# Cosine attention and a GELU layer on one core: two score passes moved in front of the next w_in stage

## The chip, the core and the metric

The kernel runs on one core of a Trainium2 chip. The metric is the time of one execution in microseconds of the device; smaller is better. The kernel before takes 417.93 us as the median of its first three runs. All runs used are fast, with a granted TensorE clock of 0.992 to 1.0.

## The reference

Shapes: q, k, v are (8 batches, 12 heads, 448 positions, 64), x is then (3584, 768), w_in (768, 2048), w_out (2048, 768).

```python
q_n = q / (np.linalg.norm(q, axis=-1, keepdims=True) + 1e-06)
k_n = k / (np.linalg.norm(k, axis=-1, keepdims=True) + 1e-06)
attn = softmax(np.matmul(q_n, k_n.transpose(0, 1, 3, 2)) / tau)      # tau = 0.1 (written out in the original)
out = np.matmul(attn, v)
x = out.transpose(0, 2, 1, 3).reshape(B * S, H * D)
h = x @ w_in
g = 0.5 * h * (1.0 + erf(h / np.sqrt(2.0)))
return g @ w_out
```

## The kernel before

One batch after the other goes through attention (`attention(b)`) and the first matmul with its gelu (`first(b)`, called the w_in stage here). The second matmul (w_out) of earlier batches is cut into single matmuls, and these *fill* the gaps of the next batch's attention: `run()` issues a number of them from a plan. The order on each engine is the order in which the program issues. (The code below leaves out loads, squares and scales.)

The profile names the work by the tiles: st is a pass of scores, pt its exps, sm the row sums, o the values, hp the w_in stage, op the w_out matmuls, nq a reduced square. "Turn" is used in two ways. A turn of TensorE is its change from one kind of matmul to another; VectorE's turn of the sums (tr) is the transpose that takes them out of their bank.

A batch has three *quads* of four heads. A quad has seven *passes*: a pass is four 64x64 matmuls into a pair of PSUM banks (`scores`) and one exp of that pair on ScalarE (`exps`). A *visit* is a few passes in a row. After a quad's seven passes come its row sums, its values and its normalising (`both`).

```python
    def both(g, p):
        sums(g)                  # TensorE, 16 matmuls into one of the two small banks
        turned(g)                # VectorE: transposes the sums out of that bank
        inverted(g)
        spread(g, 0)
        spread(g, 1)
        values(g, p=p)           # TensorE, 28 matmuls into pair p
        normalise(g, 0)          # VectorE: writes x, which the w_in stage reads
        normalise(g, 1)

    group_pairs = [(0, 1, 2), (0, 1, 2), (0, 1, 2), (1, 2), (1, 2, 0), (1, 2, 0), (2, 0), (2, 0)]
    # ... group(b, k) issues the passes of the k-th visit into these pairs ...

    def attention(b, fill):
        plan = {96: (20, 13, 13, 12, 16, 22), 128: (24, 18, 20, 18, 22, 26)}[len(fill)]
        # ...
        run()
        # ... scale and transpose the third quad ...
        group(b, 1)
        run()
        group(b, 2)
        both(g0, 0)
        group(b, 3)
        run()
        group(b, 4)
        run()
        group(b, 5)
        both(g0 + 1, 1)
        group(b, 6)
        run()
        group(b, 7)
        upto(reduce, nu + 2)     # VectorE; ScalarE's logs and roots of the next norms follow
        # ...
        run()
        both(g0 + 2, 1)
        # ...

    def first(b):
        # ...
        pairs = (0, 2) if b else (0, 2, 6, 8)     # which hp banks come from the big pairs
        ahead = 4 if b else 5                      # w_in columns begun before the last quad's x is read
        # ... 96 matmuls, 16 gelus ...
        nc.scalar.preload_act_table_set(EXP_SET)
        group(b + 1, 0)          # the first visit of the next batch: behind the w_in stage
        upto(root, 2 * b + 6)
```

The kernel uses eight PSUM banks: three pairs (0, 1, 2) and two single ones, the "small" ones, that the w_out matmuls, the sums and some w_in columns take in turn. There are 15 tiles for exps, 4 for loaded q and k, 3 for transposed quads. Batches are counted from 0. The fill has 96 matmuls in batches 1, 3, 5 and 7, and 128 in 2, 4 and 6.

Of the kernel before, what the change touches and what calls it, by code (L numbers as in the profile page):

```python
# [16 lines left out]
def kernel(  # L17
# [20 lines left out]
    NQ = H // 4  # L38
# [66 lines left out]
    def pair(i, name):  # L105
        pool = third[0] if i == 2 else ps_st
        return pool.tile([128, 2, 512], F32, tag=f"st{i}", name=name)
# [3 lines left out]

    units = [(0, 0, 1), (0, 1, 2)] + [(g, 0, 2) for g in range(1, NG)]
    NU = len(units)
    groups = [[n] for n in range(NQ + 2)] + [[NQ + 2, NQ + 3]]
    for n in range(2 * NQ + 1, NU, NQ):
        groups += [[n, n + 1], [n + 2]]
    shapes = [[len(gr), 2, units[gr[0]][2] - units[gr[0]][1], C] for gr in groups]
    place = {u: (n, j) for n, gr in enumerate(groups) for j, u in enumerate(gr)}
    qk_t, v_t, sq_t, nq_t, rn_t, qkb_t, qkT_t, pt_t = {}, {}, {}, {}, {}, {}, {}, {}
# [139 lines left out]
    def sums(g, chunks=range(C)):  # L259
        for c in chunks:  # L260
            if c == 0:
                bank_t[g, "sm"] = ps_acc.tile([128, 512], F32, tag="sm", name=f"sm{g}") if g < NQ else \
                    mm_tile(f"sm{g}", aside=0)
            for s in range(2):
                if g < NQ:
                    nc.tensor.matmul(bank_t[g, "sm"][64 * s:64 * (s + 1), :S],  # L266
                                     lhsT=ones2.rearrange("p a h r -> p (a h r)"), rhs=pt_t[g, s, c],
                                     start=(c == 0), stop=(c == C - 1), tile_position=(0, 64 * s))
                    continue

                half = 2
                for i in range(2) if c == half else ((c - (c > half)) % 2,):
                    r = 32 * (2 * s + i)
                    cols = slice(i * S // 2, (i + 1) * S // 2) if c == half else slice(0, S)
                    nc.tensor.matmul(bank_t[g, "sm"][r:r + 32, cols], lhsT=ones, rhs=pt_t[g, s, c][:, cols],  # L275
                                     start=(c < 2), stop=(c >= C - 2), tile_position=(0, r))
# [18 lines left out]
    def turned(g):  # L295
        tr = rcp.tile([128, NB, 32], F32, tag="tr", name=f"tr{g}")
        nc.vector.transpose(tr.rearrange("p b r -> p (b r)"), bank_t.pop((g, "sm"))[:, :S])  # L297
        bank_t[g, "tr"] = tr.rearrange("p b (k r) -> p k b r", k=2)

    def inverted(g):  # L300
        tr = bank_t.pop((g, "tr"))
        if g < NQ:
            su = tr[:, :, :, 0]
        else:


            for j in range(4):
                o = j ^ 1
                nc.vector.tensor_reduce(tr[32 * j:32 * (j + 1), :, :, 1], tr[32 * o:32 * (o + 1), :, :, 0:1],  # L309
                                        mybir.AxisListType.X, ALU.add)  # L310
            su = rcp.tile([128, 2, NB], F32, tag="su", name=f"su{g}")
            nc.vector.tensor_reduce(su, tr[:, :, :, 0:2], mybir.AxisListType.X, ALU.add)
        rc = bank_t[g, "rc"] = rcp.tile([128, 2, NB], F32, tag="rc", name=f"rc{g}")
        nc.vector.reciprocal(rc, su)

    def spread(g, h):
        rs = rcp.tile([128, NB, 32], F32, tag=f"rs{h}", name=f"rs{g}_{h}")
        nc.vector.transpose(rs, bank_t[g, "rc"][:, h].to_broadcast([128, NB, 32]))  # L318
        rs_t[g, h] = rs.rearrange("p b r -> p (b r)")
# [5 lines left out]
    def both(g, p):  # L325
        sums(g)
        turned(g)
# [3 lines that stand above are left out]
        values(g, p=p)  # L331
        normalise(g, 0)
        normalise(g, 1)
# [60 lines left out]
    def upto(f, n, last=None):  # L394
        last = {load_qk: NG, load_v: NV, root: len(groups), load_wi: 4, load_wo: 4}.get(f, NU)
        while done.get(f, 0) < min(n, last):
            done[f] = done.get(f, 0) + 1
            f(done[f] - 1)
# [173 lines left out]
        done.update({square: 6, reduce: 5, root: 5, scale: 5, transposes: 5})  # L572


    passes = [(n, c) for n in range(NQ) for c in range(C)]
    group_pairs = [(0, 1, 2), (0, 1, 2), (0, 1, 2), (1, 2), (1, 2, 0), (1, 2, 0), (2, 0), (2, 0)]

    def group(b, k):
        n0 = sum(len(p) for p in group_pairs[:k])
        for p, (n, c) in zip(group_pairs[k], passes[n0:]):  # L580
            scores(b * NQ + n, ((0, c), (1, c)), p)
            exps(b * NQ + n, ((0, c), (1, c)))

    def attention(b, fill):
        fill = list(fill)
        plan = {96: (20, 13, 13, 12, 16, 22), 128: (24, 18, 20, 18, 22, 26)}[len(fill)]
        parts = iter(plan)

        def run():
            for _ in range(next(parts)):  # L590
                fill.pop(0)()

        x_t[b] = xp.tile([128, KD, S], BF16, tag="x", name=f"x{b}")
        g0, nu = b * NQ, (b + 1) * NQ + 1
        run()
        for n in (nu - 1, nu):
            upto(scale, n)
            upto(transposes, n)
        group(b, 1)
        upto(square, nu + 1)  # L600
        run()
        group(b, 2)
        both(g0, 0)
        upto(load_v, b + 3)
        if b == 1:
            upto(load_qk, g0 + NQ + 2)
        group(b, 3)
        upto(square, nu + 2)
        run()
        group(b, 4)  # L610
        upto(reduce, nu + 1)
        upto(load_qk, g0 + NQ + 3)
        run()
        group(b, 5)
        both(g0 + 1, 1)
        group(b, 6)
        run()
        group(b, 7)
        upto(reduce, nu + 2)
        n = 2 * b + 4  # L620
        if n < len(groups):
            logs(n)
            roots(n)
        run()
        both(g0 + 2, 1)
        if n < len(groups):
            inverses(n)
            done[root] = n + 1

    def first(b):  # L630
        sb, hf = divmod(b, 2)
        if hf == 0:
            g_t[sb] = gp.tile([128, KF, 2 * S], BF16, tag="g", name=f"g{sb}")
        nc.scalar.preload_act_table_set(GELU_SET)
        nu = (b + 1) * NQ + 1
        hps = {}
        pairs = (0, 2) if b else (0, 2, 6, 8)
        ahead = 4 if b else 5

        def mm(m, kds):  # L640
            for kd in kds:
                nc.tensor.matmul(hps[m], lhsT=wi[:, kd, m * 128:(m + 1) * 128],  # L642
                                 rhs=x_t[b][:, kd, :], start=(kd == 0), stop=(kd == KD - 1))

        def bank(m):
            if m in pairs:
                p = (2, 0)[m // 2] if b else (1, 0, 1, 0)[pairs.index(m)]
                st = pair(p, f"hp{b}_{m}")
                hps[m], hps[m + 1] = st[:, 0, :S], st[:, 1, :S]
            elif m not in hps:  # L650
                hps[m] = mm_tile(f"hp{b}_{m}")[:, :S]

        for m in range(ahead):
            bank(m)
            mm(m, range(KD - 2))
        if b == 0:
            upto(square, nu + 3)
        for n in (nu + 1, nu + 2) if b else (nu + 1,):
            upto(scale, n)
            upto(transposes, n)  # L660
        if b:
            upto(load_qk, (b + 1) * NQ + 5)
        else:
            upto(load_wo, 4)
        upto(square, nu + 3)
        upto(reduce, nu + 3)
        for m in range(ahead):
            mm(m, range(KD - 2, KD))
        for m in range(KF):
            if b == 0 and m == 8:  # L670
                for i in range(2):
                    transposes(4, i)
                    copies(4, i)
            if m >= ahead and (m == 0 or m - 1 not in pairs):
                for k in range(m, m + 1 + (m in pairs)):
                    bank(k)
                    mm(k, range(KD))
            nc.scalar.activation(g_t[sb][:, m, hf * S:(hf + 1) * S], hps.pop(m), AF.Gelu)  # L678
            if b == 0 and m == 5:
                nc.scalar.preload_act_table_set(EXP_SET)  # L680
                upto(root, 6)
                nc.scalar.preload_act_table_set(GELU_SET)
                upto(scale, nu + 2)
                upto(transposes, nu + 2)
                upto(load_qk, 2 * NQ + 1)
        if b + 1 < B:
            nc.scalar.preload_act_table_set(EXP_SET)
            group(b + 1, 0)
            upto(root, 2 * b + 6)

    upto(load_qk, 1)
# [8 lines left out]
    fill = []  # L700
    for b in range(B):
# [12 lines left out]
        fill = [f for t, ni in todo if t not in tail for f in second_pieces(sb, t, ni)]  # L714
# [38 lines left out]
```

## Time and profile before

| Engine | busy us of 416.8 |
|---|---|
| TensorE | 409.3 |
| ScalarE | 246.6 |
| VectorE | 188.3 |
| GpSimd | 167.3 |

TensorE's "busy" is nearly the span, so it tells little about how well the engine is used: the same 12 matmuls of a visit count 0.69 us in one place and 0.82 in another. The chain of waits in order of time is of more use, because it gives each stretch of matmuls its own length. The same work can then be compared in two places, and what one of them takes longer is a wait or a turn. The prediction below shows the lines for batch 3.

### The profile page before, as it was taken

The page shows a single profiled execution, that of the slowest core. Times are in us where ns is not written, and L with a number is a line of the kernel's source. Part 1 is how long each engine was busy: PE and PEld are TensorE (multiplying, and loading weights), DVE is VectorE, ACT ScalarE, POOL GpSimd, SP SyncE. Part 2 cuts the span into 40 slices and gives each one's busy share as a digit, 9 for nine tenths or more (in the row PEclk, how much of TensorE's full clock was granted, in tenths as well). Part 3 has the DMA queues.
Part 4 walks back from the last instruction along what each step waited for, and adds up shares of the span by engine and source line. Part 5 has one row for each costly group of instructions (what it writes and reads, how often), then busy time and mean ns, then how long its engine had stood idle before and what let it go on. Part 6 is the DMA issues. An engine that isn't in the chain of part 4 may idle for free.

```text
span 416.8 us, 8254 instructions
## 1 busy us (share of the span) xinstructions
PE 409.3 (98%) x3506; PEld 212.1 (51%) x3506; DVE 188.3 (45%) x379; ACT 246.6 (59%) x358; POOL 167.3 (40%) x113
## 2 busy tenths in 40 slices
PE   7899999999999999999999999999999999999996
PEld 3344545555555554554555555455555554555564
DVE  5777228801676016741276314861167511661021
ACT  5995698356663578735865359735866348844300
POOL 4999706090900909053640636317280272000000
PEclk9999999999999999999999999999999999999999
DMA  8999999445473546729192382936375160430033
GB/s 288 263 259 205 204 215 258 115 81 186 91 185 77 92 174 92 187 60 242 18 233 65 77 228 43 195 77 126 141 135 180 38 90 0 85 75 2 0 77 76
DMA packets 66516, 54.53 MB, mean 131 GB/s; under 512 B 38576, under 2 KB 61488, under 8 KB 66480
## 3 DMA queue, kind: packets, MB, share of 16 engines
q1 hardware_dynamic: 53984, 41.79, 39.3%
q0 software_dynamic: 12112, 11.80, 17.8%
q8 instruction: 27, 0.44, 0.4%
q10 hardware_dynamic: 384, 0.43, 0.3%
q14 instruction: 9, 0.07, 0.1%
HBM read 45.61 MB, written 11.01 MB: 136 GB/s over the span
## 4 chain that ended last, share of the span: by engine, by line
PE 95%; DMA 2%; ACT 1%; DVE 1%; SPq 1%; issue 0%; DVEq 0%
PE hp L642 35%; PE op L352 35%; PE st L246 9%; PE o L289 8%; PE sm L275 4%; DMA qk<-in_q_dram 2%; PE op L367 1%; PE sm L266 1%; ACT pt L253 1%; SPq L129 1%; PE tp L225 0%; DVE qkT L230 0%; ACT sq L154 0%; DVE rn L192 0%; ACT root L178 0%
## 5 line engine op out<-in xcount | busy, mean ns | idle before, releaser
L253 ACT ACTIVATE pt<-st 128x896 bf16<-128x896 f32 x168 | 143.0, 917 | 39.6 <-PE st L246 38.7
L352 PE MATMUL op<-wo,g 128*128 128x384 bf16 x864 | 147.9, 327 | 0.0
L642 PE MATMUL hp<-x,wi 128*128 128x448 bf16 x768 | 146.8, 353 | 0.0
L678 ACT ACTIVATE g<-hp 128x448 bf16<-128x448 f32 x128 | 66.8, 547 | 99.3 <-PE hp L642 99.0
L352 PEld LDWEIGHTS <-g 128*128 128x128 bf16 x864 | 81.1, 98 | 63.2 <-issue 12.7
L642 PEld LDWEIGHTS <-wi 128*128 128x128 bf16 x768 | 74.4, 98 | 71.4 <-issue 2.9
L208 POOL TENSOR_TENSOR qkb<-qk,rn 128x896 bf16<-128x896 f32 (+1 forms) x49 | 79.7, 1652 | 47.1 <-DVE rn L192 47.1
L165 DVE TENSOR_REDUCE nq<-sq 128x28 f32<-128x1792 f32 (+2 forms) x30 | 48.8, 1637 | 64.6 <-POOL sq L156 61.3
L156 POOL TENSOR_TENSOR sq<-qk 128x1792 f32<-128x1792 f32 (+1 forms) x22 | 66.8, 3042 | 12.9 <-DMA qk<-in_k_dram 12.7
L356 DVE COPY ot<-op 128x384 f32<-128x384 f32 x54 | 29.5, 547 | 69.6 <-PE op L352 69.6
L190 POOL TENSOR_SCALAR se<-sr 128x28 f32<-128x28 f32 (+1 forms) x14 | 4.4, 313 | 122.7 <-ACT sr L181 122.7
L246 PE MATMUL st<-qkT 64*64 64x448 bf16 x672 | 48.3, 359 | 1.2 <-DVE qkT L230 1.0
L289 PE MATMUL o<-pt,v 64*64 64x448 bf16 x672 | 36.9, 352 | 0.0
L246 PEld LDWEIGHTS <-qkT 64*64 64x64 bf16 x672 | 18.2, 105 | 26.6 <-issue 18.3
L192 DVE RECIPROCAL rn<-se 128x28 f32<-128x28 f32 (+2 forms) x18 | 6.8, 376 | 51.4 <-POOL se L190 51.1
L318 DVE STREAM_TRANSPOSE rs<-rc 128x448 f32<-128x448 f32 x48 | 28.1, 623 | 0.8
L297 DVE STREAM_TRANSPOSE tr<-sm 128x448 f32<-128x448 f32 x24 | 15.6, 649 | 28.5 <-PE sm L275 25.4
L323 DVE TENSOR_TENSOR x<-o,rs 128x448 bf16<-128x448 f32 x48 | 27.0, 600 | 1.0 <-DVE rs L318 0.5
L289 PEld LDWEIGHTS <-v 64*64 64x64 bf16 x672 | 17.7, 106 | 15.8 <-issue 7.2
L275 PE MATMUL sm<-pt,ones 128*32 128x448 bf16 (+1 forms) x336 | 19.3, 332 | 0.0
L309 DVE TENSOR_REDUCE tr<-tr 32x28 f32<-32x28 f32 x84 | 16.5, 196 | 1.6
L275 PEld LDWEIGHTS <-ones 128*32 128x32 bf16 x336 | 7.4, 95 | 10.6 <-issue 8.9
(43 smaller groups left out, 118.5 us busy)
## 6 DMA issues: line engine op xcount, KB each, us to landing
out_dram<-ot SPq DMA_DIRECT2D x54, 192.0 KB, 2.7
qk<-in_q_dram SPq DMA_DIRECT2D x23, 448.0 KB, 6.3
qk<-in_k_dram SPq DMA_DIRECT2D x23, 448.0 KB, 7.0
v<-in_v_dram POOLq DMA_DIRECT2D x7, 672.0 KB, 10.8
wi<-in_moe_w_in_dram POOLq DMA_DIRECT2D x8, 384.0 KB, 14.3
wo<-in_moe_w_out_dram POOLq DMA_DIRECT2D x4, 768.0 KB, 14.0
qk<-in_q_dram SPq DMA_DIRECT2D x2, 224.0 KB, 3.6
v<-in_v_dram POOLq DMA_DIRECT2D x1, 448.0 KB, 9.5
```

The costliest lines, as they stand in the source:

```text
L156: eng.tensor_tensor(sq[:, part], t[:, part], t[:, part], ALU.mult)
L165: nc.vector.tensor_reduce(nq[:, part], sq[:, part], mybir.AxisListType.X, ALU.add)
L208: eng.tensor_tensor(qkb[:, i, :, s0:s1].rearrange("p c s d -> p s c d"), t[:, i, s0:s1], rn[:, i].to_broadcast([128, s1 - s0, C, D]), ALU. ...
L246: nc.tensor.matmul(st[cols, n, :S], lhsT=qkT[rows, 1, c, cols], rhs=qkT[rows, 0, :, cols], start=True, stop=True, tile_position=(64 * s, 6 ...
L253: nc.scalar.activation(pt[:, :m], st[:, :m, :S], AF.Exp, scale=inv_tau)
L275: nc.tensor.matmul(bank_t[g, "sm"][r:r + 32, cols], lhsT=ones, rhs=pt_t[g, s, c][:, cols], start=(c < 2), stop=(c >= C - 2), tile_position ...
L289: nc.tensor.matmul(bank_t[g, h][cols, :S], lhsT=v_t[g][rows, s, c, :], rhs=pt_t[g, s, c][rows], start=(c == 0), stop=(c == C - 1), tile_po ...
L318: nc.vector.transpose(rs, bank_t[g, "rc"][:, h].to_broadcast([128, NB, 32]))
L352: nc.tensor.matmul(ps[:, :NH], lhsT=g_t[sb][:, kf, t * 128:(t + 1) * 128], rhs=wo[:, kf, ni * NH:(ni + 1) * NH], start=(kf == 0), stop=(kf ...
L356: nc.vector.tensor_copy(ot[:, ni * NH:(ni + 1) * NH], ps[:, :NH])
L642: nc.tensor.matmul(hps[m], lhsT=wi[:, kd, m * 128:(m + 1) * 128], rhs=x_t[b][:, kd, :], start=(kd == 0), stop=(kd == KD - 1))
L678: nc.scalar.activation(g_t[sb][:, m, hf * S:(hf + 1) * S], hps.pop(m), AF.Gelu)
```

## The change

Intent: from the fourth batch on, two score passes of a batch are issued before the w_in stage of the batch in front of it, right behind that batch's last values. The visit behind the w_in stage goes, the other visits are spread anew among the w_out matmuls, and the norms and transposes run one quad further ahead. The w_in stage takes other banks first, and begins six columns instead of four before it reads the last quad.

```diff
-    groups = [[n] for n in range(NQ + 2)] + [[NQ + 2, NQ + 3]]
-    for n in range(2 * NQ + 1, NU, NQ):
-        groups += [[n, n + 1], [n + 2]]
+    groups = [[n] for n in range(NQ + 2)] + [[NQ + 2, NQ + 3], [2 * NQ + 1, 2 * NQ + 2]]
+    for n in range(3 * NQ, NU, NQ):
+        groups += [[n, n + 1], [n + 2]] if n + 2 < NU else [[n]]
 ...
-        plan = {96: (20, 13, 13, 12, 16, 22), 128: (24, 18, 20, 18, 22, 26)}[len(fill)]
+        plan = {96: (16, 14, 16, 18, 16, 16), 128: (20, 18, 20, 22, 32, 16)}[len(fill)]
 ... attention(b), visits, runs and sums alone:
-        run(); group(b, 1); run(); group(b, 2); both(g0, 0); group(b, 3); run()
-        group(b, 4); run(); group(b, 5); both(g0 + 1, 1); group(b, 6); run(); group(b, 7)
-        run(); both(g0 + 2, 1)
+        run(); visit(b, (0, 1, 2)); run(); visit(b, (0, 1, 2)); run()
+        visit(b, (0, 1) if b <= 2 else (0, 1, 2)); run()
+        visit(b, (0, 1, 2)); both(g0, 0); visit(b, (1, 2)); run()
+        visit(b, (1, 2, 0)); both(g0 + 1, 1); visit(b, (2, 0)); run()
+        both(g0 + 2, 2)
+        if b > 1:
+            visit(b + 1, (0, 1))
 ... first(b):
-        pairs = (0, 2) if b else (0, 2, 6, 8)
-        ahead = 4 if b else 5
+        pairs = {2: 0, 4: 1} if b else {0: 1, 2: 0, 6: 1, 8: 0}
+        ahead = 6 if b else 5
 ...
-            group(b + 1, 0)
+            if b <= 1:
+                visit(b + 1, (0, 1, 2))
```

(The lines of the attention are drawn together here; the loads, squares, reduces and scales between them move too.)

More of the change, by code (lines that the diff above doesn't have):

```diff
@@ L575, with visit @@
     passes = [(n, c) for n in range(NQ) for c in range(C)]
-    group_pairs = [(0, 1, 2), (0, 1, 2), (0, 1, 2), (1, 2), (1, 2, 0), (1, 2, 0), (2, 0), (2, 0)]
-    def group(b, k):
-        n0 = sum(len(p) for p in group_pairs[:k])
-        for p, (n, c) in zip(group_pairs[k], passes[n0:]):
+    at = {}
+    def visit(b, pairs):
+        for p in pairs:
+            n, c = passes[at.get(b, 0)]
+            at[b] = at.get(b, 0) + 1
             scores(b * NQ + n, ((0, c), (1, c)), p)
@@ L593, in attention @@
         x_t[b] = xp.tile([128, KD, S], BF16, tag="x", name=f"x{b}")
-        g0, nu = b * NQ, (b + 1) * NQ + 1
+        g0, u = b * NQ, b * NQ + 1
         run()
-        for n in (nu - 1, nu):
-            upto(scale, n)
-            upto(transposes, n)
-        group(b, 1)
-        upto(square, nu + 1)
-        run()
-        group(b, 2)
+        upto(scale, u + 3)
+        upto(transposes, u + 3)
+        if b == 1:
+            upto(load_qk, g0 + NQ + 2)
+            upto(square, u + 4)
+        visit(b, (0, 1, 2))
+        if b > 1:
+            upto(scale, u + 4)
+            upto(transposes, u + 4)
+        run()
+        visit(b, (0, 1, 2))
+        run()
+        upto(load_qk, g0 + NQ + 3)
+        visit(b, (0, 1) if b <= 2 else (0, 1, 2))
+        upto(square, u + 5)
+        run()
+        visit(b, (0, 1, 2))
         both(g0, 0)
         upto(load_v, b + 3)
-        if b == 1:
-            upto(load_qk, g0 + NQ + 2)
-        group(b, 3)
-        upto(square, nu + 2)
+        upto(load_qk, g0 + NQ + 4)
+        visit(b, (1, 2))
+        upto(reduce, u + 4 + (b > 1))
         run()
-        group(b, 4)
-        upto(reduce, nu + 1)
-        upto(load_qk, g0 + NQ + 3)
-        run()
-        group(b, 5)
+        visit(b, (1, 2, 0))
         both(g0 + 1, 1)
-        group(b, 6)
-        run()
-        group(b, 7)
-        upto(reduce, nu + 2)
+        visit(b, (2, 0))
+        upto(reduce, u + 5)
         n = 2 * b + 4
@@ L624, in attention @@
         run()
-        both(g0 + 2, 1)
+        both(g0 + 2, 2)
         if n < len(groups):
@@ L628, in attention @@
             done[root] = n + 1
+            if b > 1:
+                visit(b + 1, (0, 1))
     def first(b):
@@ L634, in first @@
         nc.scalar.preload_act_table_set(GELU_SET)
-        nu = (b + 1) * NQ + 1
+        u = (b + 1) * NQ + 1
         hps = {}
-        pairs = (0, 2) if b else (0, 2, 6, 8)
-        ahead = 4 if b else 5
+        pairs = {2: 0, 4: 1} if b else {0: 1, 2: 0, 6: 1, 8: 0}
+        ahead = 6 if b else 5
         def mm(m, kds):
@@ L646, in bank @@
             if m in pairs:
-                p = (2, 0)[m // 2] if b else (1, 0, 1, 0)[pairs.index(m)]
-                st = pair(p, f"hp{b}_{m}")
+                st = pair(pairs[m], f"hp{b}_{m}")
                 hps[m], hps[m + 1] = st[:, 0, :S], st[:, 1, :S]
@@ L656, in first @@
         if b == 0:
-            upto(square, nu + 3)
-        for n in (nu + 1, nu + 2) if b else (nu + 1,):
-            upto(scale, n)
-            upto(transposes, n)
-        if b:
+            upto(square, u + 3)
+            upto(scale, u + 1)
+            upto(transposes, u + 1)
+            upto(load_wo, 4)
+            upto(reduce, u + 3)
+        else:
+            upto(scale, u + 2)
+            upto(transposes, u + 2)
             upto(load_qk, (b + 1) * NQ + 5)
-        else:
-            upto(load_wo, 4)
-        upto(square, nu + 3)
-        upto(reduce, nu + 3)
+            upto(square, u + 4)
+            upto(reduce, u + 4)
         for m in range(ahead):
@@ L682, in first @@
                 nc.scalar.preload_act_table_set(GELU_SET)
-                upto(scale, nu + 2)
-                upto(transposes, nu + 2)
+                upto(scale, u + 2)
+                upto(transposes, u + 2)
                 upto(load_qk, 2 * NQ + 1)
```

## The prediction

> **What bounds the kernel now.** I read the page's engine table first (TensorE busy 409.3 of 416.8 us at a granted clock of 0.998), then the chain of waits by line, then the same chain in order of time.
>
> ```profile
> PE 95%; DMA 2%; ACT 1%; DVE 1%; SPq 1%; issue 0%; DVEq 0%
> PE hp L642 35%; PE op L352 35%; PE st L246 9%; PE o L289 8%; PE sm L275 4%; DMA qk<-in_q_dram 2%; PE op L367 1%; PE sm L266 1%; ACT pt L253 1%; SPq L129 1%; PE tp L225 0%; DVE qkT L230 0%; ACT sq L154 0%; DVE rn L192 0%; ACT root L178 0%
> ```
>
> The chain is TensorE from 19 us to the end, so time comes only from what stands between one matmul and the next on that engine. The number of matmuls does not change (3506). What can change is how often TensorE turns from one kind of matmul to another and where it waits for a bank. The chain in time shows both. Here is batch 3 (counting from 0), columns start us, length us, what:
>
> ```profile
> 131.99 18.27 PE hp L642 x96
> 150.26 0.69 PE st L246 x12
> 150.95 3.36 PE op L352 x20
> 154.31 0.82 PE st L246 x12
> 155.12 2.22 PE op L352 x13
> 157.34 0.72 PE st L246 x12
> 158.06 0.98 PE sm L275 x16
> 159.04 1.45 PE o L289 x28
> 160.49 0.38 PE st L246 x8
> 160.87 2.22 PE op L352 x13
> 163.09 0.79 PE st L246 x12
> ...
> 171.98 0.50 PE st L246 x8
> ...
> 176.16 0.78 PE sm L275 x16
> ```
>
> Three things are to be seen. First, a price of turning: two passes (8 matmuls) cost 0.38 us right behind the values (o, the same 64x64 tiling) and 0.50 us behind w_out matmuls (op, 128x128): 0.12 us for the turn. In the same chain 13 op matmuls take 2.22 us and 26 take 4.33 us, so one is 0.162 us and the turn into op 0.11 us; 96 op matmuls behind the w_in stage (hp, also 128x128) take 15.60 us, which is 0.1625 each and no turn at all. Second, waits: three passes cost 0.69 us when nothing is short, but 0.82, 0.72 and 0.79 us in this batch. Third, the first row sums (sm) of a batch take 0.98 us, the later ones 0.78 us.
>
> ScalarE's timeline tells why (start, length, what):
>
> ```profile
> 150.86 1.28 ACT L687 ACT_TABLE_LOAD   x1
> 152.15 2.54 ACT L253 ACTIVATE pt<-st 128x896 bf16<-128x896 f32 x3
> 154.56 0.33 ACT L172 ACTIVATE lq<-nq,tiny 128x28 f32<-128x28 f32 x1
> 155.11 5.13 ACT L253 ACTIVATE pt<-st 128x896 bf16<-128x896 f32 x6
> ```
>
> The first visit's scores are ready at 151, but the last gelu and the table load hold its exps until 152.15; they free the third pair of banks only near 154.7, and the second visit, begun at 154.31, has to wait for it. Its own exps wait for the logs and run into the third visit's (six in a row). The sums need seven passes; the seventh is the first of the third visit, started 0.7 us earlier, and its exp ends about 0.2 us too late.
>
> **What the Trainium skill says.** "TensorEngine Tiling (Array Packing)", Key Properties: changing the tiling mode drains the TensorE. The trace agrees: 0.11 to 0.12 us a change, nothing from o to st or from hp to op. "ScalarE: Activation LUTs", What ACT_TABLE_LOAD costs: about 1283 ns for a load; the trace has 1.28. "PSUM — Partial Sum Buffer", Engine vs sequencer instructions: VectorE's queue is strict FIFO; the trace agrees in that its rows never overtake the built order, and my loss below rests on it.
>
> **The change, part by part.** (a) In batches 3 to 7 the visit behind the w_in stage is gone. Two of its passes stand behind the last values of the batch before, and hp runs straight into op. Counting turns per batch: 19 before, 17 after; five batches, so 10 x 0.12 = 1.2 us.
>
> (b) The first sums come after four visits (14 passes from batch 3 on), not after three: all seven exps are long done. 0.20 to 0.23 us in each of seven batches: 1.5 us.
>
> (c) The run of op between visits is 14 to 18 in the batches with 96 op matmuls (1, 3, 5, 7), where it was 12, 13 and 13, and the exps that start a batch are no longer behind a table load. In batches 3, 5 and 7 the 0.13 + 0.03 + 0.10 us of waits go: 0.8 us. In exchange the two-pass visit behind the first values gets as close to its exps as the one behind the second values is now, which takes 0.42 us and not 0.38: 0.04 x 7 = 0.3 us lost.
>
> (d) Batches 1 and 2 keep the visit behind w_in, now with only 16 and 20 op behind it (20 and 24 before). Its exps end 4.5 us after w_in. In batch 1 the next visit starts 0.69 + 2.71 = 3.4 us after w_in and waits 0.6 us for its third pair; in batch 2, 0.1 us.
>
> Summing the pieces with the durations above gives these stretches from w_in to w_in: 46.40 us becomes 45.77 in batches 3 and 5 and 45.39 in batch 7 (whose two passes left and which sends none ahead); 51.37 becomes 51.68 in batch 2 (it takes in two passes) and 50.97 in batches 4 and 6. Batches 2 to 7: 293.31 before, 290.55 after, 2.76 us won. Batch 1 up to its w_in stage: 28.13 becomes 28.3.
>
> (e) The hidden part. The w_in stage now takes its first two banks from the two small ones, and the last row sums stand in the very bank that it takes first. So it cannot start before VectorE has turned those sums. VectorE's timeline of batch 1 before the change:
>
> ```profile
> 74.44 2.00 DVE L165 TENSOR_REDUCE nq<-sq 128x28 f32<-128x1792 f32 x1
> 76.36 0.55 DVE L356 COPY ot<-op 128x384 f32<-128x384 f32 x1
> 78.43 0.56 DVE L356 COPY ot<-op 128x384 f32<-128x384 f32 x1 [1.52 <-PE op L352]
> 79.22 0.65 DVE L297 STREAM_TRANSPOSE tr<-sm 128x448 f32<-128x448 f32 x1 [0.23 <-PE sm L275]
> ```
>
> Now there is slack (the brackets: idle time before the row, and what ended it): 38 op matmuls lie between the second values and the last sums. After the change there are 16. In batch 1 a reduce still stands in between. I follow VectorE's order from the first sums' end at an estimated 68.0 us. Turn and normalise take 4.29 us to the next start, reduce 1.92, copy 0.55, so the second turn starts near 74.8, although its sums ended at 74.0. Then 4.29, reduce 1.92, copy 0.5: the third turn runs from 81.5 to 82.15. TensorE is through with the values at 80.85 and waits 1.35 us. With the 0.2 us from (d), batch 1 loses 1.6 us. From batch 2 on the second of these reduces is gone (one stands behind the first values, two in the w_in stage). In batch 3 the third turn then ends about 1.0 us before w_in needs the bank. Normalising the last quad also stays ahead: 24 instead of 16 matmuls run before it is needed.
>
> Net: -2.76 + 1.6 = -1.2 us.
>
> **Rivals.** First, the wait in (e) doesn't arise or isn't this long: then about 415.3 us. For it: ready times are estimates. Against: the built order has TensorE wait for VectorE at the first hp matmul, and before the change it doesn't. Second, (e) also bites in batches 3, 5 and 7. The slack is only 1.0 us, and a reduce that starts late would bring it back; 1 us in each would give 419.8. Against: that reduce's square comes from GpSimd about 5 us before it is wanted. Third, the exp waits of (b) and (c) only move, so that turns alone are won: 417.9 - 1.2 + 1.6 = 418.3. Against: after w_in ScalarE has its logs behind it at 2.6 us, and the first visit comes no sooner. Fourth, a buffer runs short. Fourteen exp tiles are outstanding before the first values, of 15; that fits, but a late release would stop ScalarE. The quad ahead needs its turned tile's buffer, free after the second visit, and a transfer that took 2.6 us before with over 10 us to spare: hidden.
>
> **Range and chances.** From the median of 417.93 us I predict 416.7. The gain of 2.8 is a sum of small terms, each good to about a third; the loss is one term, between 0.5 and 2. Eight times in ten: 415.0 to 418.2. Two per cent is 8.4 us; no rival gets there short of a deadlock-like wait in every batch. Faster by over 2%: 0.01; within 2%: 0.97; slower: 0.02.
>
> **What would show it.** In the chain of the changed kernel: no st between hp and op from batch 3 on; every three-pass visit there at 0.69; every first sum at 0.78; the stretches 45.8 and 51.0 us; a w_in stage of batch 1 that starts near 82.2 us, with a gap before it that ends on VectorE's turn of the sums. I am wrong if such gaps come in later batches, if sums stay at 0.98, or if batch 1 starts its w_in stage near 80.8.

## The result, and the profile after

The changed kernel takes 416.97 us (median of six runs, 416.80 to 417.30), the kernel before 418.16 us in the six runs beside it. The ratio is 0.9971, with a 95% interval of 0.9958 to 0.9984. By the limit of 2% that is "same"; the interval lies below one, so a small gain is there.

The chain of waits of the changed kernel in order of time, batch 3 (start us, length us, what):

```profile
151.60 2.60 PE op L352 x16
154.20 0.69 PE st L246 x12
154.89 2.38 PE op L352 x14
157.28 0.69 PE st L246 x12
...
164.40 0.69 PE st L246 x12
165.09 0.78 PE sm L275 x16
165.87 1.45 PE o L289 x28
167.31 0.42 PE st L246 x8
...
178.70 0.38 PE st L246 x8
179.08 18.27 PE hp L649 x96
```

The w_out matmuls stand right behind the w_in stage, which ended at 151.60, and 16 of them take 2.60 us, 0.1625 each, so that join is free of a turn. Every visit of three passes takes 0.69 us. The first sums take 0.78. The two passes ahead cost 0.38 us behind the values.

Batch 1 looks different. TensorE's timeline there, with the idle time before a row in brackets:

```profile
55.23 0.72 PE L246 MATMUL st<-qkT 64*64 64x448 bf16 x8
56.38 0.38 PE L246 MATMUL st<-qkT 64*64 64x448 bf16 x4 [0.43 <-ACT pt L253]
...
78.92 1.52 PE L289 MATMUL o<-pt,v 64*64 64x448 bf16 x28
81.61 4.70 PE L649 MATMUL hp<-x,wi 128*128 128x448 bf16 x24 [1.16 <-DVE tr L297]
```

and VectorE's timeline of the same place:

```profile
78.54 2.00 DVE L165 TENSOR_REDUCE nq<-sq 128x28 f32<-128x1792 f32 x1
80.45 0.54 DVE L356 COPY ot<-op 128x384 f32<-128x384 f32 x1
80.92 0.63 DVE L297 STREAM_TRANSPOSE tr<-sm 128x448 f32<-128x448 f32 x1
```

The sums had ended near 79.0 us, when the values began. VectorE turned them out of their bank only at 80.92, because a reduce and a copy stood in front of the turn in its queue. The w_in stage wanted that bank next, and TensorE stood still for 1.16 us. VectorE was late before that: the chain of waits of this batch runs on VectorE from 67.60 us, the turn of the first sums, to 81.56, with no pause over 0.39 us, and it holds two such reduces, at 71.96 and 78.61.

To compare batch by batch, I took TensorE's timeline and read off the time from the end of one w_in stage to the start of the next. It is free of the first 32 to 34 us, which differ by up to two microseconds between executions of any of these kernels. (Ends of matmuls are modelled, and neighbouring rows overlap by 0.06 us; that is the same in all.) Six of the experiments are in the table already; each is described below.

| batch | 1 | 2 | 3 | 4 | 5 | 6 | 7 | sum |
|---|---|---|---|---|---|---|---|---|
| before | 28.07 | 33.04 | 28.06 | 33.04 | 28.06 | 33.04 | 28.05 | 211.36 |
| changed | 29.71 | 33.34 | 27.41 | 32.61 | 27.41 | 32.60 | 27.03 | 210.11 |
| batch1_old | 28.37 | 33.33 | 27.41 | 32.61 | 27.41 | 32.62 | 27.03 | 208.78 |
| visit_behind_w_in | 29.72 | 32.97 | 28.41 | 32.96 | 28.42 | 32.96 | 28.42 | 213.86 |
| sums_one_early | 27.94 | 32.84 | 27.89 | 32.84 | 27.88 | 32.84 | 27.87 | 210.10 |
| extra_turns | 30.44 | 33.81 | 27.87 | 33.06 | 27.87 | 33.07 | 27.50 | 213.62 |
| thirteen_tiles | 29.71 | 33.40 | 27.47 | 32.67 | 27.47 | 32.68 | 27.09 | 210.49 |
| batch1_new_order | 27.80 | 33.34 | 27.41 | 32.61 | 27.41 | 32.61 | 27.03 | 208.21 |

So batches 2 to 7 win 2.89 us (183.29 to 180.40), batch 1 loses 1.64, and 1.25 us are left. The spans of the two profiled executions differ by more, 416.8 and 414.9 us: another 0.6 us of it lies before the first w_in stage, which began at 33.37 us in one and at 32.79 in the other. That part of the program is the same in both.

### The profile page after: what moved, and what is told of

It reads as the page before. It is cut to its first block, busy times and chain, and to the rows that moved or that the text cites. A ratio compares the mean times of both kernels' runs of the same rounds, so it can differ in the third digit from the quotient of the medians.

```text
span 414.9 us, 8256 instructions
## 1 busy us (share of the span) xinstructions
PE 406.9 (98%) x3506; PEld 212.5 (51%) x3506; DVE 188.5 (45%) x379; ACT 246.3 (59%) x358; POOL 166.9 (40%) x113
## 4 chain that ended last, share of the span: by engine, by line
PE 93%; DVE 4%; ACT 2%; issue 0%
PE hp L649 35%; PE op L352 33%; PE st L246 9%; PE o L289 7%; PE sm L275 4%; PE spin L403 2%; ACT pt L253 1%; PE op L367 1%; PE sm L266 1%; DVE nq L165 1%; PE tp L225 1%; DVE x L323 1%; DVE tr L297 0%; DVE tr L309 0%; DVE rs L318 0%
## 5 line engine op out<-in xcount | busy, mean ns | idle before, releaser
L685 ACT ACTIVATE g<-hp 128x448 bf16<-128x448 f32 x128 | 65.9, 545 | 68.3 <-PE hp L649 68.0
L156 POOL TENSOR_TENSOR sq<-qk 128x1792 f32<-128x1792 f32 (+1 forms) x22 | 66.5, 3035 | 13.5 <-DMA qk<-in_k_dram 13.5
L275 PE MATMUL sm<-pt,ones 128*32 128x448 bf16 (+1 forms) x336 | 17.8, 332 | 0.0
L403 PE MATMUL spin<-blank,ident 128*128 128x448 bf16 x34 | 10.0, 442 | 2.2 <-DVE root L89 1.9
```

The costliest lines, as they stand in the source:

```text
L156: eng.tensor_tensor(sq[:, part], t[:, part], t[:, part], ALU.mult)
L275: nc.tensor.matmul(bank_t[g, "sm"][r:r + 32, cols], lhsT=ones, rhs=pt_t[g, s, c][:, cols], start=(c < 2), stop=(c >= C - 2), tile_position ...
L685: nc.scalar.activation(g_t[sb][:, m, hf * S:(hf + 1) * S], hps.pop(m), AF.Gelu)
```

## The experiments

Eight kernels ran; one was wrong. The kernel before was timed beside them on the same chip (median 418.29 us in the first lot and 418.31 in the second).

### same_again

Edit: none; the changed kernel itself.

> The changed kernel once more, as the yardstick for the runs beside it. Ratio to the kernel before 0.997; the w_in stage of batch 1 starts 29.7 us after that of batch 0 ended, with a gap of about 1.2 us before it that ends on VectorE's turn of the last row sums. If the gap was an accident of one execution, it is gone here.

Measured: 416.59 us (416.32 to 419.43), ratio 0.9977 (0.9956 to 0.9997). The wait in front of the w_in stage of batch 1 is there again, 1.17 us, and ends on VectorE's turn. The stretches of batches 2 to 7 repeat those of the first execution within 0.02 us. But the stretch of batch 1 was 30.91 us and not 29.7. The trace shows a second wait in this execution: the second pass of the third visit found its transposed quad late and cost another 1.2 us; TensorE's weight load there reads

```profile
61.94 0.14 PEld L246 LDWEIGHTS <-qkT 64*64 64x64 bf16 x8 [1.27 <-DMA qkT<-qkb]
```

The DMA engines are busy throughout that stretch, with other loads in both queues. The two transposes in it took 13.2 and 13.5 us to land. In the executions without this wait they took 10.6 to 12.1, the first of the changed kernel among them; those between 130 and 235 us of the kernel before have a median of 4.1. The batch1_old and extra_turns executions show the same wait with 0.2 to 0.3 us (transposes of 11.9 to 13.0 us). So it varies from execution to execution, and in these traces it is seen in batch 1 only. Why the transposes take so long there is not shown.

### batch1_old

```diff
+    def attention_one(b, fill):     # visits, runs (20, 13, 13, 12, 16, 22), sums and pairs as before the change
+        ...
+        both(g0 + 2, 1)
 ...
-        pairs = {2: 0, 4: 1} if b else {0: 1, 2: 0, 6: 1, 8: 0}
-        ahead = 6 if b else 5
+        pairs = {0: {0: 1, 2: 0, 6: 1, 8: 0}, 1: {0: 2, 2: 0}}.get(b, {2: 0, 4: 1})
+        ahead = {0: 5, 1: 4}.get(b, 6)
 ...
-            attention(b, fill)
+            (attention_one if b == 1 else attention)(b, fill)
```

> Batch 1 alone in the arrangement of the kernel before (visits, runs of op 20/13/13/12/16/22, last values in pair 1, w_in into pairs 2 and 0 first); all other batches as changed. My theory: what batch 1 lost comes back whole, 28.1 us from w_in to w_in and not 29.7, so 1.5 us less than the changed kernel, ratio to before about 0.9933. Rival: what batch 1 wins is given back in batch 2, whose scores wait for something that batch 1 had delayed (a load, a square), and the ratio stays at 0.997.

Measured: 414.94 us (414.69 to 416.35), ratio 0.9928 (0.9916 to 0.9939). Batch 1 is back at 28.37 us, of which 0.3 are the late transpose just told, and batches 2 to 7 keep what they had won. The rival falls: nothing is given back later. It beats both kernels.

### reduce_behind_turn

```diff
         visit(b, (2, 0))
-        upto(reduce, u + 5)
-        # logs and roots here
         run()
-        both(g0 + 2, 2)
+        sums(g); turned(g)
+        upto(reduce, u + 5); logs(n); roots(n)
+        inverted(g); spread(g, 0); spread(g, 1)
+        values(g, p=2); normalise(g, 0); normalise(g, 1)
```

(in batch 1 alone; g is its third quad)

> The changed kernel with one thing moved: in batch 1 the second reduce (and the logs behind it) stands behind VectorE's turn of the last row sums instead of in front of the last run of op. My theory: the wait is the queue's order and not the amount of VectorE's work, so the turn starts as its sums end, near 79.0, and w_in starts right behind the values; normalising ends no earlier than now, and TensorE reaches the last quad just as it is ready: 1.0 to 1.2 us less than the changed kernel, ratio about 0.994. Rival: VectorE's sum of work is the limit, and the wait only moves from the first w_in matmul to the matmul that reads the last quad: same time as the changed kernel.

Measured: 415.77 us (415.28 to 418.57), ratio 0.9962 (0.9940 to 0.9984). The interval is wide, and the ratio alone doesn't tell this kernel from the changed one (0.9977 beside it). The trace does. VectorE's timeline of batch 1:

```profile
78.56 0.65 DVE L297 STREAM_TRANSPOSE tr<-sm 128x448 f32<-128x448 f32 x1
79.13 1.98 DVE L165 TENSOR_REDUCE nq<-sq 128x28 f32<-128x1792 f32 x1
```

and TensorE's:

```profile
78.43 1.52 PE L289 MATMUL o<-pt,v 64*64 64x448 bf16 x28
79.88 18.57 PE L664 MATMUL hp<-x,wi 128*128 128x448 bf16 x96
```

The turn starts as the sums end, and the w_in stage begins behind the values without a gap: the stretch of batch 1 is 28.48 us. The w_in stage takes 18.57 us and not 18.33, because the last quad's x, whose normalising the reduce now delays, comes a little late: part of the wait has moved on, as the rival said, but only 0.24 us of it. From the end of the w_in stage of batch 0 to the end of that of batch 1 the chain has 98.45 - 51.42 = 47.03 us, against 99.93 - 51.91 = 48.02 in the changed kernel. The theory stands with 1.0 us: it was the order in VectorE's queue, and the amount of its work holds back a fifth of what the order gives.

### visit_behind_w_in

```diff
-        visit(b, (0, 1) if b <= 2 else (0, 1, 2))
+        visit(b, (0, 1))
 ...
-            if b > 1:
-                visit(b + 1, (0, 1))
 ...
-            if b <= 1:
-                visit(b + 1, (0, 1, 2))
+            visit(b + 1, (0, 1, 2))
```

> The changed kernel without passes ahead: every batch has its first visit of three passes behind the w_in stage as batches 1 and 2 have; all else (runs of op, sums after the fourth visit, banks) as changed. My theory: five batches get two turns back (10 x 0.12 = 1.2 us) and the second visit waits for the exps behind the table load, as batches 1 and 2 show: 0.77 us in batches 3, 5 and 7, 0.12 in 4 and 6, 2.5 us. Together 3.7 us more than the changed kernel, ratio to before about 1.006. Rival: the passes ahead are worth only their turns and the waits were already cured by the longer runs: 1.2 us more, ratio 1.000.

Measured: 420.36 us (420.13 to 421.71), ratio 1.0057 (1.0045 to 1.0068). The table gives 3.75 us more than the changed kernel. TensorE's timeline at the second visit of batch 3:

```profile
154.24 0.72 PE L246 MATMUL st<-qkT 64*64 64x448 bf16 x8
155.39 0.38 PE L246 MATMUL st<-qkT 64*64 64x448 bf16 x4 [0.43 <-ACT pt L253]
```

The third pass waits for the exps that stood behind the table load, just as in batch 1. So the passes ahead are worth far more than their turns. Without them the rest of the change makes batches 3, 5 and 7 slower than they were before (28.41 against 28.06 us), since fewer w_out matmuls now stand between the first visit and the second.

### sums_one_early

```diff
-    ... lhsT=ones, rhs=pt_t[g, s, c][:, cols], ...
+    src = c - 1 if g % NQ == 0 and c == C - 1 else c
+    ... lhsT=ones, rhs=pt_t[g, s, src][:, cols], ...
```

(on the kernel before)

> The kernel BEFORE, with a wrong result on purpose: the first row sums of each batch from 1 on take the sixth pass's exps a second time in place of the seventh's, so they need not wait for the third visit's exp; nothing else changes. My theory of part (b): the first sums go from 0.98 and 1.01 to 0.78 us in seven batches, the visit behind them from 0.38 to 0.42: 1.2 to 1.5 us less than the kernel before, ratio 0.9965 to 0.997. Rival: the wait only moves to the values, which need a pair of banks that the same exp frees: ratio 1.000.

Measured: wrong (relative error 0.026), 416.89 us (416.42 to 417.02), ratio 0.9971 (0.9956 to 0.9985). The chain of waits in batch 3:

```profile
156.11 0.72 PE st L246 x12
156.84 0.78 PE sm L276 x16
157.61 1.45 PE o L290 x28
```

The sums fell from 0.98 to 0.78 us, and the values behind them stayed at 1.45. The visit behind the values took 0.39 us here and 0.42 in batch 6; 0.42 was expected. The table has 1.26 us less in all, 0.18 a batch. So the wait was for that one exp and did not move to the values. The wait in the visit ahead of the sums (0.72 here and in the kernel before) is left as it was.

### extra_turns

```diff
-        plan = {96: (16, 14, 16, 18, 16, 16), 128: (20, 18, 20, 22, 32, 16)}[len(fill)]
+        plan = {96: (16, 14, 15, 17, 16, 16), 128: (20, 18, 19, 21, 32, 16)}[len(fill)]
 ...
-        visit(b, (0, 1, 2))
+        visit(b, (0,))
+        fill.pop(0)()
+        visit(b, (1, 2))
```

(the same again at the third visit)

> The changed kernel with one op matmul put between the first and the second pass of the second and of the third visit of each batch (taken from the run behind): the same matmuls, 4 turns more a batch, 28 in all. My theory: 0.12 us a turn, 3.3 us more than the changed kernel, ratio to before about 1.005. Rival: turns are an artefact of how the trace models the ends of matmuls, and cost nothing: ratio 0.997.

Measured: 420.25 us (419.68 to 423.23), ratio 1.0063 (1.0040 to 1.0086). The chain in batch 3:

```profile
159.81 0.31 PE st L246 x4
160.12 0.27 PE op L352
160.39 0.50 PE st L246 x8
160.89 2.54 PE op L352 x15
```

One op matmul between two turns takes 0.27 us, the turn into it included; in a stream it takes 0.16. A visit of three passes is 0.81 us in two pieces (0.31 + 0.50) and 0.69 in one. The table gives 3.51 us for 28 turns, or 0.125 us each, but batch 1 has the late transpose in it; in batches 2 to 7, where no other wait is seen, 2.78 us for 24, or 0.116. The measured time rose too, so turns are real time of the device and not of the trace's model alone.

### thirteen_tiles

```diff
-    ptp = ctx.enter_context(tc.tile_pool(name="ptp", bufs=15))
+    ptp = ctx.enter_context(tc.tile_pool(name="ptp", bufs=13))
```

> The changed kernel with 13 exp tiles in place of 15. It has 14 exps outstanding before the first values of a batch. My theory: the third exp of the fourth visit has no tile until those values are done, 0.9 us later than now, and the second pass behind them waits for its pair: 0.85 us in each of seven batches, 6 us more than the changed kernel, ratio about 1.011. Rival: an exp that late is hidden by the run of op behind it: ratio 0.997.

Measured: 417.45 us (416.72 to 419.20), ratio 0.9989 (0.9971 to 1.0007); its time does not tell it from the changed kernel. I missed this one: the table has 0.38 us more and not 6. The stall that I expected behind the first values is absent; only the visit behind the second values takes 0.48 us and not 0.42, in batches 2 to 7. I had taken it that a tile comes free when all 28 value matmuls are done. But by the program the first tile is read last by the first of their seven chunks, so it can come free near the start of the values: by estimate 0.69 + 0.78 + 1.45 / 7 = 1.7 us after the start of the fourth visit, while the exp that wants it starts 2.05 us after it (0.43 to the first exp, then two pitches of 0.81). The trace bears this out in part. In batch 3 the three exps of the fourth visit run without a break while the values are at work:

```profile
164.44 2.53 ACT L253 ACTIVATE pt<-st 128x896 bf16<-128x896 f32 x3 [1.19 <-PE st L246]
165.47 1.52 PE L289 MATMUL o<-pt,v 64*64 64x448 bf16 x28
```

The third exp thus starts near 166.06, and the values end near 166.99: it had a tile before they were done. That it was the first chunk that freed it is worked out from the program; no run of its own shows it. Nor did I follow up the 0.06 us.

### batch1_new_order

```diff
+    def attention_one(b, fill):
+        parts = iter((20, 14, 14, 14, 14, 20))
+        ...
+        run(); visit(b, (0, 1, 2)); run(); visit(b, (0, 1, 2)); run(); visit(b, (0, 1, 2))
+        both(g0, 0); visit(b, (1, 2)); upto(reduce, u + 4); run()
+        visit(b, (1, 2, 0)); both(g0 + 1, 1); visit(b, (2, 0)); run()
+        visit(b, (2, 0)); upto(reduce, u + 5); logs(6); roots(6); run()
+        both(g0 + 2, 2)
```

(batch 1 alone; the banks of its w_in stage stay those of the change)

> A version meant to beat both: the changed kernel, with batch 1 in an order of its own (visits of 3, 3, 3, 3 passes, sums, 2, 3, sums, 2, 2 with runs of op 20, 14, 14, 14, 14, 20; the new banks of the w_in stage kept). Both reduces have time before the last sums, and the first sums come after four visits. From w_in to w_in in batch 1 27.7 us (28.1 in the arrangement of before, 29.7 as changed): 2.0 us less than the changed kernel, ratio 0.992. If the wait at the w_in stage were due to its new banks as such and not to the reduce in front of the turn, it would stay, and the time with it, near 0.995.

Measured: 414.85 us (414.52 to 415.52), ratio 0.9923 (0.9908 to 0.9937). Batch 1 takes 27.80 us. The chain at its end:

```profile
77.63 0.78 PE sm L275 x16
78.40 1.45 PE o L289 x28
79.85 18.27 PE hp L690 x96
```

No wait is left in front of the w_in stage, although it takes the same bank as in the changed kernel. So the new banks alone cost nothing here; the wait came with a full queue on VectorE as well. This version beats both kernels. It is not told apart from batch1_old by its time: the intervals overlap.

## Why the prediction was right

The 416.7 us stands beside 416.97 measured, within the range, and -1.2 us beside -1.19 between the medians. By its steps:

- **(a) turns.** Two turns fewer in five batches at 0.12 us. extra_turns measured 0.12 us a turn on its own. Shown.
- **(b) first sums.** 1.5 us were forecast for the sums alone, and 0.3 lost at the next visit, booked under (c): 1.2 net. sums_one_early measured 1.26 us net for this wait.
- **(c) waits of the visits.** Every visit of three passes is at 0.69 in batches 3 to 7, and the one behind the first values at 0.42, as forecast. visit_behind_w_in shows what keeps the second visit so: with the visit behind the w_in stage its wait returns.
- **(d) batches 1 and 2.** The wait in the second visit of batch 1 was forecast as 0.6 us and measured as 0.77 (from 55.31, when the run of op ended, to 56.77, less 0.69). The wait itself was right, 0.6; a pass that starts on an idle engine then took 0.38 us where one in a stream takes 0.19. The Trainium skill states something like it in "TensorE: Matmul & The Clock Gate", Single matmul latency: a lone matmul, there one over the full 128x128 array, pays a constant of about 166 ns warm besides its columns. The trace has 0.19 us for a pass of four 64x64 matmuls; that both have the same cause is not shown by a run here.
- **Stretches.** Between w_in stages the forecast was a gain of 2.76 us in batches 2 to 7; the table has 2.89. (The prediction's own parts (a) to (d), taken for these six batches, add up to about 2.9.)
- **(e) the hidden part.** Forecast: a wait of 1.35 us ending on VectorE's turn, in batch 1 only. (The sum as written, 82.15 less 80.85, is 1.30; 0.05 more lies between the turn's end and the first matmul, and the trace has that too, 81.56 to 81.61.) Measured: 1.16 us, there, and in no other batch. Together with (d), batch 1 lost 1.64 us against 1.6 forecast. That this fits so well is partly luck: without the gap batch 1 takes 28.48 us, in reduce_behind_turn, against 28.07 before the change, so some 0.4 us belong to (d), where 0.2 were forecast, and some 1.2 to the gap, where 1.35 were; the two misses cancel. Two experiments show the cause: moving the reduce behind the turn closes the gap with the banks left as they are, and batch1_new_order closes it with the reduce left in front, but with 34 w_out matmuls and not 16 between the second values and the last sums.

Of the rivals, the second (the wait spreads to batches 3, 5 and 7) and the third (the exp waits only move) are refuted by the table. The fourth was right to be set aside, but the count of 14 tiles was not what made it safe: thirteen_tiles loses only 0.38 us with 13. The first did not come true, since the wait arose; its 415.3 us are near what a repaired batch 1 gives, 415.77 in reduce_behind_turn and 414.94 in batch1_old.

## What to carry to other kernels

When one engine is busy all the time, read the same stretch of work in two places of the chain: the difference is a turn or a wait, and here such terms added up to a forecast good to a few tenths of a microsecond. When a change hands a bank to a new user, look at who must empty it, and what stands in front of that instruction in that engine's queue. Here a single reduce in front of a turn, in a single batch, took back about a third of the 2.89 us that the other batches had won (1.0 us came back when it was moved), and putting that one batch in another order more than doubled what the change was worth.

## What the Trainium skill lacked or had wrong

- "TensorEngine Tiling (Array Packing)", Key Properties, says that a change of tiling mode drains TensorE but gives no price. It is 0.12 us a change (2.78 us for 24 in batches 2 to 7 of extra_turns), between streams of matmuls of 384 and 448 columns; 64x64 scores behind 64x64 values cost none.
- No page that I read says when a tile that a group of matmuls reads in chunks comes free: with its own last reader or with the group. Here 13 exp tiles in place of 15 cost 0.38 us over the kernel, where a release at the end of the values would have cost about 6 by my estimate, and an exp that needed such a tile started some 0.9 us before the values ended (166.06 and 166.99).
- "PSUM — Partial Sum Buffer", Engine vs sequencer instructions, says that VectorE's queue is strict FIFO. What follows for banks is not said: a reduce of 1.9 us that reads no PSUM at all held a bank, and with it TensorE for 1.16 us.
